# LSH attention and gated MLP on one core: first loads split and reordered, two raw buffers, w_sg and w_out loads held for batch 1

## The chip, the core and the metric

One core of one Trainium2 chip runs the whole kernel. The metric is device microseconds (us) for one execution, as the median of several runs. TensorE (PE) multiplies matrices, VectorE (DVE), ScalarE (ACT) and GpSimd (POOL) work on elements, SyncE (SP) mostly issues DMAs. Each engine executes its own instructions in the order in which they stand in the program, and waits on the others by semaphores.

## The reference, cut

```
q_bits = (einsum('bhsd,dk->bhsk', q, proj) > 0)      # 6 bits; the same for k
mask   = q_bucket[..., :, None] == k_bucket[..., None, :]
scores = where(mask, scale * q @ k.T, -1e9)          # 4 batches, 8 heads, 768 x 768, d 64
attn   = softmax(scores) @ v
x      = attn, heads side by side                    # 4 x 768 x 512
h      = gelu_tanh(x @ w_in); u, v = halves(h)       # 512 -> 2 x 512
v_n    = normalise(v) * g_ln
v_s    = w_sg @ v_n + b_sg                           # over the sequence, 768 x 768
out    = x + (u * v_s) @ w_out
```

All of it is in 32-bit floats.

## The kernel before, in words

**Attention.** The 32 heads are taken as 16 pairs (two heads of 64 columns fill the 128 partitions). For a pair n, `load` fetches q and k (192 KB per head and operand), `values` fetches v, `parts` transposes q and k on PE and splits each into a high and a low part (ACT `h`, DVE `l`), `features` multiplies with the projection matrix and turns signs into the bucket features `f`, `largest` computes a first score and DVE takes the row maxima `mx`, `shift` writes them into the features, and `weigh` computes the scores again in three products, with ACT taking the exponential into a ring of p tiles. The 768 queries of a pair go in two phases (256 and 512 columns). GpSimd, or DVE for some steps of the last pair (`LASTADDS`), adds the p tiles up into `sum`; PE multiplies p with v into `av`. `finish` takes the total of a phase over partitions, sends it through DRAM (s, sq), takes the reciprocal on DVE, sends that through DRAM again (r, rs) and scales: GpSimd `xt`, then DVE `xt`, then the store to `xs`. So 32 phases pass through four DMAs each. The number in a name is the phase: `xt_28` and `sum_56/57` are pair 14's first phase, `xt_30`, `sum_60/61` pair 15's first, `xt_31`, `sum_62/63` the very last. While attention runs, 16 weight jobs (`weight_job`, one row block of w_in each, with the port shared by DVE and GpSimd in mind) prepare w_in in `wflat`.

**Gated MLP.** For each of 4 batches `hidden_v` and `hidden_u` multiply x with w_in in a seven-product scheme: `prepare_ops` splits seven sums of blocks into high and low parts (x into op0 to op6, w_in into w0 to w6), `multiply` runs the products. `gate` and `project` follow for the four batches. w_sg is loaded by `gate_raw` in six groups of four transposing DMAs into one buffer `stg`, each followed by a transposition on DVE; w_out by `out_weights` in eight weight jobs. The op tiles op0 and op1 lie in memory that is free before attention ends; op2 to op6 and the output tiles lie where p tiles and v were, so they wait for attention's last sums.

**What sets the order.** Every piece of work is put into a `Plan` with an engine, an estimated cost and a priority (a number near to a time); `Plan.order` simulates the engines once while the program is built, and emits the instructions in the order of that simulation. A change of a number in the tables at the head of the file (`MX` for the MLP, `AVP`, `WARMUP`, `JOB0` and others for attention) therefore moves instructions on all engines. PE begins with fillers, multiplications of the identity with itself into an unused bank (L683, `WARMUP` of them), placed wherever the simulation sees PE idle in the first microseconds.

The lines that the change touches most: L308 loads `proj`; L469 loads q and k; L479 loads v; L631 adds p tiles; L660 to L665 are the four DMAs of `finish`; L816 makes low parts of w and op; L838 is a product of `hidden_v` or `hidden_u`, L861 a load of x, L902 a load of w_sg, L949 and L999 copies of a product out of its bank.

Of the kernel before, what the change touches and what calls it, by code (L numbers as in the profile page):

```python
# [9 lines left out]
F32 = mybir.dt.float32  # L10
F32R = mybir.dt.float32r
# [10 lines left out]
MX = {'base': 340.0, 'gs': False, 'norm': 'ACT', 'mul': ('DVE', 'POOL', 'POOL', 'POOL', 'DVE', 'POOL', 'POOL', 'DVE'), 'wg': -14.0, 'z0': -2.76, 'ox': -9.0, 'oz': -10.89, 'sp': -10.51, 'ro': -10.87, 'gr': 41.0, 'lx': 7.81, 'lz': -3.23, 'gap': 0.59, 'wo': -58.22, 'ws': 8.72, 'ul': 19.73, 'wi': -125.28, 'x0': -59.43, 'lox': ('DVE', 'DVE', 'DVE', 'DVE', 'DVE', 'DVE', 'DVE'), 'loz': ('DVE', 'DVE', 'POOL', 'DVE', 'DVE', 'DVE', 'DVE'), 'log': ('DVE', 'DVE', 'DVE', 'POOL'), 'low': ('DVE', 'POOL', 'DVE', 'DVE', 'DVE', 'DVE', 'DVE')}  # L22

AVP = 9.58
GY, GX, NPT = (3,), (3, 3), 22
NAV = 1
S0P = 0.39
AHEAD = 8
PREP, SHIFTP, FINP, WSTEP, WP = 0.64, -0.32, 3.66, 14.6, 13.44
# [3 lines left out]
FIRSTP, FIRSTS, FIRSTQ, LATE = -2.54, 2.51, -8.5, 5.81  # L33
LOAD0 = 1.35
PARTP = 1.03
VP, MARK, WARMUP = -20.0, 2, 40
X0P = 313.74
LASTADDS = ["POOL", "POOL", "DVE", "DVE", "DVE"]
AHEAD1 = 3.78
JOB0, JOBS = 1, 115  # L40
# [3 lines left out]
class Plan:  # L44
# [73 lines left out]
    def order(self):  # L118
# [32 lines left out]
        while len(out) < len(G):  # L151
# [14 lines left out]
            t0, e = min((max(when(n), since(n)), e) for e, rs in ready.items() for n in rs if early(n))  # L166
# [77 lines left out]
def kernel(  # L244
# [179 lines left out]
    if True:  # L424
# [36 lines left out]
        def load(n, prio):  # L461
            st = Pair()
            st.n, st.b, st.hp = n, *divmod(n, NP)
            st.raw = []
            for s, (nm, src) in enumerate((("q", q), ("k", k))):
                t = early.ring([P, NT, 2, D], F32, nm, 1)
                for j in range(2):
                    def fn(eng, t=t, j=j, src=src):
                        eng.dma_start(t()[:, :, j, :], src[st.b, 2 * st.hp + j].rearrange("(t p) d -> p t d", p=P))  # L469
                    dma(prio + 0.2 * s, 1.09 if n else LOAD0, fn, w=[(t, j)], e=ACT if n == 0 and s else LOADS)  # L470
# [15 lines left out]
        def parts(st, i, prio):  # L486
# [20 lines left out]
            plan.add(PE, 0.48, prio, tr, [st.raw[s] for s, _ in keys] + [(t, x) for t in (hh, lo) for x in keys] + gate, [tp], form="full")  # L507
# [128 lines left out]
        def finish(st, ph, prio):  # L636
# [4 lines left out]
            h, W = n // 2, n // 64  # L641
            sm, e = late.ring([P, NY], F32, "sm", 3), ps_tile() if st.n < NPAIR - 1 else late.ring([P, WIDE], F32, "e", 2)
# [129 lines left out]
    def w_slot(s):  # L772
        return (r0 if s < 3 else r1).ring([P, NT * HN], F32R, f"w{s}")

    def prepare_ops(left, blk, order, dst, n, a, prio, step, lo_eng):
# [49 lines left out]
    def multiply(order, ni, nc_, lhs, rhs, n, bufs, prio, step, done):  # L825
        a, b, c = {}, {}, {}
        for s, k in enumerate(order):
            group = {1: a, 6: a, 7: a, 4: a, 5: b, 3: b, 2: c}[k]
            for i in range(ni):
# [11 lines left out]
                plan.add(PE, 3 * nc_ * n * 0.0004525, prio + s * step + 0.01 * i, mm, bufs(s), [ps])  # L841
# [25 lines left out]
    def in_weights(prio):  # L867
        w = {s: w_slot(s) for s in range(7)}
        wf = lambda: wflat[:, :NC * FF].rearrange("p (a b) -> p a b", a=NC)
        for u in range(2):  # L870
# [10 lines left out]
            prepare_ops(False, [blk(j, k) for j in range(2) for k in range(2)], GORDER, dst, 512, 2, prio + 8 * u, 1.0, LOW)  # L881
# [11 lines left out]

    def gate_raw(prio):
        wt = plan.buf("wraw", 1)
        sg = w_sg.rearrange("(a b) s -> b a s", b=32)
        for t in range(NT):
            st = r2.ring([P, S], F32, "stg")
            for g in range(4):
# [3 lines left out]
                dma(prio + 3 * t, 0.65, fn, w=[(st, g)])  # L903
# [33 lines left out]
    def hidden_v(b, ops, w, prio, step):  # L937
# [54 lines left out]
        multiply(GORDER, 3, 2, lhs, rhs, QN, lambda s: [(ops[s], 0), (ops[s], 1), (w[s], (0, 0)), (w[s], (0, 1))], prio, step, done)  # L992
# [170 lines left out]
    wi = in_weights(T + M_["wi"])  # L1163
    blk = load_x(0, T + M_["x0"])
    g_col, b_bc = vectors(T + 30)
    for b in range(B):
# [6 lines left out]
        if b == 0:  # L1173
            wt = gate_raw(T + M_["gr"])
# [52 lines left out]
```

## Time and profile before

| | us |
|---|---|
| median of 3 runs | 756.45 (754.81, 756.45, 757.75) |
| the profiled execution, whole | 749.46 |
| its span, first to last instruction | 747.7 |
| TensorE busy in it | 721.7 |

The profiled execution is 7.0 us shorter than the median of the runs; what lies around its span is 1.76 us. Where a row below says how long something takes, it is from that one execution. A line of the timeline view joins instructions of one kind that follow each other: start, length, engine, line, operation, output <- input, count, and in brackets how long the engine had been idle and who released it.

### The profile page before, as it was taken

The numbers are of one execution on the slowest core, as the hardware profiler recorded it, in microseconds if no ns is written. First come the engines' busy times: TensorE is split into PE (matmuls) and PEld (weight loads), VectorE is DVE, ScalarE is ACT, GpSimd is POOL, SyncE is SP. The second block draws the span as 40 slices with busy tenths as digits, with TensorE's granted clock in tenths as the row PEclk, the third lists the DMA queues.
The fourth block names the chain that finished last, engine by engine and source line by source line (L and its number), as shares of the span: only waits on it lengthen the run. The fifth ranks groups of instructions, "written<-read, shape, count | busy, mean of one in ns | idle before, by whom it ended". The sixth has DMA issues, their size and how long they took to land.

```text
span 747.7 us, 16648 instructions
## 1 busy us (share of the span) xinstructions
PE 721.7 (97%) x6396; PEld 579.3 (77%) x6396; DVE 557.7 (75%) x1022; ACT 361.0 (48%) x697; POOL 379.0 (51%) x355
## 2 busy tenths in 40 slices
PE   8999999999999799999999978899999999999997
PEld 8677667676767566867676648899999989999896
DVE  4896878789788989778975967769899845445443
ACT  2355546554655354655565746758769221202010
POOL 0267669678866756967886750211314521304020
PEclk9999999999999899999999998899999999999999
DMA  5333442442344043244122335576544756474534
GB/s 112 74 69 92 96 98 58 112 111 62 99 101 117 21 108 80 79 109 113 26 66 64 89 72 141 156 215 245 191 156 161 244 144 186 104 205 99 143 75 113
DMA packets 200272, 86.04 MB, mean 115 GB/s; under 512 B 171264, under 2 KB 179584, under 8 KB 200192
## 3 DMA queue, kind: packets, MB, share of 16 engines
q1 hardware_dynamic: 197088, 84.18, 43.2%
q10 hardware_dynamic: 3104, 0.80, 0.5%
q8 instruction: 50, 0.82, 0.5%
q14 instruction: 30, 0.25, 0.1%
HBM read 59.48 MB, written 25.36 MB: 113 GB/s over the span
## 4 chain that ended last, share of the span: by engine, by line
PE 74%; DVE 13%; DMA 5%; ACT 3%; issue 3%; POOL 2%; SPq 0%; DVEq 0%; ACTq 0%; POOLq 0%
PE g L596 16%; PE g L1105 13%; PE av L619 10%; PE g L1151 9%; PE g L543 8%; PE g L838 5%; PE g L518 5%; PE av L622 3%; PE g L497 2%; DMA rs<-r 2%; PE g L651 2%; DVE mx L551 1%; PE ftp L683 1%; POOL sum L631 1%; DVE wy L349 1%
## 5 line engine op out<-in xcount | busy, mean ns | idle before, releaser
L601 ACT ACTIVATE p<-g 128x512 f32<-128x512 f32 x288 | 157.4, 599 | 65.0 <-PE g L596 57.1
L631 POOL TENSOR_TENSOR sum<-sum,p 128x512 f32<-128x512 f32 x154 | 183.4, 1226 | 4.1 <-ACT p L601 4.1
L551 DVE TENSOR_REDUCE mx<-g 128x1 f32<-128x512 f32 x192 | 122.7, 684 | 32.7 <-PE g L543 27.9
L631 POOL TENSOR_TENSOR sum<-p,p 128x512 f32<-128x512 f32 x64 | 83.8, 1326 | 87.0 <-ACT p L601 87.0
L1105 PE MATMUL g<-w,op 128*128 128x384 f32 x576 | 100.7, 334 | 0.0
L1105 PEld LDWEIGHTS g<-w,op 128*128 128x128 f32 x576 | 100.0, 188 | 0.2
L619 PE MATMUL av<-p,v 128*32 128x512 f32 x768 | 88.1, 594 | 1.3 <-ACT un L657 1.3
L553 DVE TENSOR_REDUCE mx<-g 128x2 f32<-128x512 f32 x96 | 61.5, 683 | 27.3 <-PE g L543 24.2
L596 PE MATMUL g<-h 64*128 64x256 f32 (+1 forms) x384 | 75.4, 350 | 5.6 <-DVE xt L673 5.0
L838 PE MATMUL g<-w,op 128*128 128x256 f32 x504 | 64.9, 291 | 7.6 <-ACT out L949 5.8
L596 PE MATMUL g<-h,l 64*128 64x256 f32 (+1 forms) x384 | 72.2, 338 | 0.0
L596 PE MATMUL g<-f 64*128 64x256 f32 (+1 forms) x384 | 71.4, 336 | 0.2 <-DMA f<-m 0.2
L838 PEld LDWEIGHTS g<-w,op 128*128 128x128 f32 x504 | 63.5, 198 | 10.0 <-ACT out L949 6.3
L596 PE MATMUL g<-l,h 64*128 64x256 f32 (+1 forms) x384 | 71.1, 335 | 0.0
L543 PE MATMUL g<-f 64*128 64x512 f32 (+1 forms) x384 | 68.8, 347 | 1.0 <-DVE f L523 0.9
L838 PE MATMUL g<-op,w 128*128 128x384 f32 x336 | 64.0, 348 | 3.9 <-ACT out L999 3.4
L1073 POOL TENSOR_TENSOR out<-out,ul 128x384 f32<-128x384 f32 x20 | 20.3, 1017 | 93.4 <-issue 49.9
L543 PE MATMUL g<-h 64*128 64x512 f32 (+1 forms) x384 | 66.6, 336 | 0.0
L672 POOL TENSOR_TENSOR xt<-un,rs 128x256 f32<-128x256 f32 (+1 forms) x32 | 34.3, 1073 | 61.7 <-DMA rs<-r 44.1
L838 PEld LDWEIGHTS g<-op,w 128*128 128x128 f32 x336 | 60.6, 196 | 6.3 <-ACT out L999 5.4
L596 PEld LDWEIGHTS g<-h 64*128 64x128 f32 x384 | 41.8, 187 | 24.2 <-DVE xt L673 5.9
L1151 PE MATMUL g<-woh,op 128*128 128x512 f32 x192 | 59.8, 389 | 0.0
(127 smaller groups left out, 1287.4 us busy)
## 6 DMA issues: line engine op xcount, KB each, us to landing
q<-in_q_dram SPq DMA_DIRECT2D x32, 192.0 KB
v<-in_v_dram SPq DMA_DIRECT2D x16, 384.0 KB
raw<-xs SPq DMA_DIRECT2D x16, 384.0 KB
vn<-out SPq DMA_DIRECT2D x24, 256.0 KB
ud<-out SPq DMA_DIRECT2D x16, 384.0 KB
stg<-xs SPq DMA_DIRECT2D x96, 64.0 KB
ul<-ud SPq DMA_DIRECT2D x32, 192.0 KB
raw<-vn SPq DMA_DIRECT2D x8, 768.0 KB
```

What stands on the lines that cost most here:

```text
L518: nc.tensor.matmul(fp()[:, c * n:(c + 1) * n], w[:, s, :], x()[:, s, cs], start=(u == 0), stop=(u == 2))
L543: nc.tensor.matmul(sc[j]()[:, c * NY:c * NY + b - a], x()[row(j), 0, qs], x()[row(j), 1, a:b], start=(n == 0), stop=(n == 1))
L551: nc.vector.tensor_reduce(mx()[:, 0, i0 + w, j:j + 1], sc[j]()[:, :WIDE], axis=AX.X, op=ALU.max, negate=True)
L553: nc.vector.tensor_reduce(mx()[:, 1, i0:i0 + 2, j], two(sc[j]()), axis=AX.X, op=ALU.max, negate=True)
L596: nc.tensor.matmul(sc[j]()[:, i * w:(i + 1) * w], x()[row(j), 1, ks], y()[row(j), 0, cs], start=(m == 0), stop=(m == 3))
L601: plan.add(ACT, 0.6, prio, lambda j=j: nc.scalar.activation(p[j]()[:, :, :NY], two(sc[j]()), AF.Exp, scale=SCALE), [sc[j]], [p[j]])
L619: nc.tensor.matmul(two(av())[rows(j, a)], st.v()[:, j, x, cols(a)], ps[x][j]()[:, :, :NY], start=(x == 0), stop=(x == 5))
L631: (nc.gpsimd if e == POOL else nc.vector).tensor_add(two(sums[j]()), a, p[j]()[:, :, :NY])
L672: plan.add(POOL, 0.13 + n / 420.0, prio + TAILP, lambda: nc.gpsimd.tensor_mul(xt()[:, :n], un()[:, :n], rs()[:, :n]), [un, rs], [xt])
L838: nc.tensor.matmul(ps()[:, :n], lhs(s, i, ci, x, y), rhs(s, i, ci, x, y), start=(first and ci == 0 and x + y == 0), stop=(ci == nc_ - 1 an ...
L1105: nc.tensor.matmul(ps()[:, :HN], a()[:, x, c0:c0 + P], c()[:, 3 * HN * y + ci * HN:3 * HN * y + (ci + 1) * HN], start=(j == 0 and ci == 0 ...
L1151: nc.tensor.matmul(ps(), a()[:, x, c0:c0 + P], w()[:, 2 * j + ci, :], start=(j == 1 and ci == 0 and x == 0 and w is th), stop=(j == 0 and ...
```

## The change

- **Loads of the first pair.** `proj` is issued by GpSimd's queue instead of SP's. q of pair 0 is loaded in two parts (column tiles 0 and 1, then 2 to 5). ACT's function table is loaded early, by a dummy operation (`warm`).
- **Rings.** q and k have two buffers (`RAWS`) instead of one, and a transposition waits for the halves that it reads. The ring of p tiles has 19 entries instead of 22.
- **Layout.** k and v are read so that one partition holds six consecutive rows (1536 B in a run) instead of rows 128 apart (256 B in a run). The keys are thereby permuted, in k and v alike.
- **Fillers.** 30 instead of 40, and other priorities for the first pairs.
- **w_sg and w_out.** Both wait for buffers `began`: their first loads may be issued when the first product of batch 1 has begun. `gate_raw` is called in batch 1's turn.
- **w_in.** w0 to w2 are prepared as before; the splits for w3 to w6 have priorities of their own (`wj`), later.
- **Last pair.** Its first addition of the second phase goes to DVE instead of GpSimd (`LASTADDS`); the planner takes its DRAM round trips as 1.5 us longer (`TRIP`), which changes the order only.
- **Engines.** Three of seven low parts of x (`lox`: third, sixth, seventh) go to GpSimd, none of w_in's; other tables are retuned.

```diff
-GY, GX, NPT = (3,), (3, 3), 22
+TRIP = 1.5
+RAWS, LATEQ, PRQ = 2, 4.0, True
+GY, GX, NPT = (3,), (3, 3), 19
...
-VP, MARK, WARMUP = -20.0, 2, 40
+VP, MARK, WARMUP = -20.0, 2, 30
...
-LASTADDS = ["POOL", "POOL", "DVE", "DVE", "DVE"]
+LASTADDS = ['DVE', 'POOL', 'DVE', 'DVE', 'DVE']
...
-JOB0, JOBS = 1, 115
+JOB0, JOBS = 2, 114
...
+    warm = const.tile([P, 1], F32, name="warm")
+    nc.scalar.mul(warm, small, 1.0)
     for j in range(2):
-        nc.sync.dma_start(pr[j * D:(j + 1) * D], proj)
+        (nc.gpsimd if PRQ else nc.sync).dma_start(pr[j * D:(j + 1) * D], proj)
...
-                t = early.ring([P, NT, 2, D], F32, nm, 1)
...
+                t = early.ring([P, NT, 2, D], F32, nm, RAWS)
+                for ts in ((slice(0, 2), slice(2, NT)) if n + s == 0 else (slice(0, NT),)):
+                    for j in range(2):
...
+                            order = "(p t) d -> p t d" if src is k else "(t p) d -> p t d"
...
-                st.v(), v[st.b, 2 * st.hp:2 * st.hp + 2].rearrange("j (t p) d -> p j t d", p=P)),
+                st.v(), v[st.b, 2 * st.hp:2 * st.hp + 2].rearrange("j (p t) d -> p j t d", t=NT)),
...
-            prepare_ops(False, [blk(j, k) for j in range(2) for k in range(2)], GORDER, dst, 512, 2, prio + 8 * u, 1.0, LOW)
+            prepare_ops(False, [blk(j, k) for j in range(2) for k in range(2)], GORDER, dst, 512, 2, [prio + s + 8 * u if s < M_["r0n"] else T + M_["wj"] + 15 * u + 2.1 * s for s in range(7)], 0.0, LOW)
...
-                dma(prio + 3 * t, 0.65, fn, w=[(st, g)])
+                dma(prio + 3 * t, 0.65, fn, [began[M_["grb"]]], [(st, g)])
...
-                       lambda x=x: x(), x, p, JOBC)
+                       lambda x=x: x(), x, p, JOBC, [began[M_["wob"]]])
...
-        if b == 0:
+        if b == M_["grb"]:
             wt = gate_raw(T + M_["gr"])
```

Three places in the order show what this does.

**ACT's first instructions** (`k_0` is pair 0's k, `pr` the projection matrix, `pw` its arrangement, `h0_0` the high part of pair 0). Before:

```order
L469 DMA k_0_266<-in_k_dram 128x6x64 x2
L409 ACT_TABLE_LOAD
L409 ACTIVATE pw_117<-pr_73 64x6 x8
L412 CAST pwh_127<-pw_117 128x256
L501 CAST h0_0_299<-g0_850_289 128x2x256
```

After:

```order
L475 DMA k_0_262<-in_k_dram 128x6x64
L310 ACT_TABLE_LOAD
L310 ACTIVATE warm_74<-small_69 128x1
L413 ACTIVATE pw_119<-pr_73 64x6 x4
L475 DMA k_0_262<-in_k_dram 128x6x64
L413 ACTIVATE pw_119<-pr_73 64x6 x4
L416 CAST pwh_129<-pw_119 128x256
L509 CAST h0_0_291<-g0_850_281 128x2x256
```

The second half of k now stands behind four operations that read `pr`.

**GpSimd at the end of attention.** Before:

```order
L631 TENSOR_TENSOR sum_60_6758<-p12_168,p14_170 128x512
L631 TENSOR_TENSOR sum_61_6782<-p13_169,p15_171 128x512
L672 TENSOR_TENSOR xt_28_6823<-un_28_6445,rs_28_6736 128x256
L631 TENSOR_TENSOR sum_60_6758<-sum_60_6758,p0_156 128x512
L631 TENSOR_TENSOR sum_61_6782<-sum_61_6782,p1_157 128x512
L631 TENSOR_TENSOR sum_62_6863<-p6_162,p16_172 128x512
L631 TENSOR_TENSOR sum_63_6884<-p7_163,p17_173 128x512
L631 TENSOR_TENSOR sum_62_6863<-sum_62_6863,p2_158 128x512
L631 TENSOR_TENSOR sum_63_6884<-sum_63_6884,p3_159 128x512
```

After:

```order
L639 TENSOR_TENSOR sum_60_6590<-p16_174,p1_159 128x512
L639 TENSOR_TENSOR sum_61_6595<-p0_158,p2_160 128x512
L639 TENSOR_TENSOR sum_60_6590<-sum_60_6590,p3_161 128x512
L681 TENSOR_TENSOR xt_27_6670<-un_27_6233,rs_27_6592 128x512
L639 TENSOR_TENSOR sum_61_6595<-sum_61_6595,p4_162 128x512
L681 TENSOR_TENSOR xt_28_6737<-un_28_6407,rs_28_6655 128x256
L639 TENSOR_TENSOR sum_62_6725<-sum_62_6725,p13_171 128x512
L639 TENSOR_TENSOR sum_63_6765<-sum_63_6765,p14_172 128x512
```

`xt_28` moved behind the sums of pair 15's first phase, and two additions left the engine.

**SP's queue behind pair 15's totals** (`stg` from `in_moe_w_sg_dram` is w_sg, `raw_1` batch 1's x). Before:

```order
L902 DMA stg_2_6916<-in_moe_w_sg_dram 32x24x32 x4
L665 DMA rs_29_6940<-r_14_1_259 128x1x512
L664 DMA r_15_0_261<-sq_30_6906 128x4
L861 DMA raw_1_6973<-xs_1_94 128x768 x4
L902 DMA stg_3_7003<-in_moe_w_sg_dram 32x24x32
L665 DMA rs_30_7013<-r_15_0_261 128x1x256
L902 DMA stg_3_7003<-in_moe_w_sg_dram 32x24x32 x3
```

After, and then the place where w_sg now begins:

```order
L674 DMA rs_30_6936<-r_15_0_257 128x1x256
L673 DMA r_15_1_259<-sq_31_6907 128x8
L872 DMA raw_1_6971<-xs_1_96 128x768 x4
L684 DMA xs_3_98<-xt_30_6983 128x256
L674 DMA rs_31_7020<-r_15_1_259 128x1x512
```

```order
L915 DMA stg_0_7254<-in_moe_w_sg_dram 32x24x32 x4
L1035 DMA ud_0_103<-out1_0_6901 128x768 x3
L348 DMA ow64_0_7311<-in_moe_w_out_dram 128x512
L1035 DMA ud_0_103<-out1_0_6901 128x768
L1083 DMA ul_0_7341<-ud_0_103 128x384
L915 DMA stg_1_7350<-in_moe_w_sg_dram 32x24x32 x4
L872 DMA raw_2_7377<-xs_2_97 128x768 x4
```

All six groups of w_sg moved behind the last pair's round trips, and two of them now stand ahead of batch 2's x.

## Rows read from the trace of the kernel before

**Rows 1.** The page: busy us, share of span, instructions by engine

```profile
PE 721.7 (97%) x6396; PEld 579.3 (77%) x6396; DVE 557.7 (75%) x1022; ACT 361.0 (48%) x697; POOL 379.0 (51%) x355
```

**Rows 2.** Windows: length, PE, PEld, DVE, ACT, POOL busy, clock, DMA share, GB/s

```profile
420.00:460.00 40.00, 32.28 (x297) 24.62 (x298) 32.14 (x39) 23.48 (x47) 19.88 (x13) 0.91 0.34 70
460.00:500.00 40.00, 35.79 (x234) 34.29 (x235) 27.76 (x61) 25.96 (x52) 7.15 (x9) 0.91 0.60 171
```

**Rows 3.** Timeline of the start, all engines

```profile
0.74 1.22 SPq L308 DMA_DIRECT2D pr<-in_proj_dram  x2
0.74 1.03 ACTq L469 DMA_DIRECT2D k<-in_k_dram  x2
...
2.79 6.96 PE L683 MATMUL ftp<-ident 128*128 128x128 f32 x34 [0.26 <-DVE fcol L401]
3.71 1.28 ACT L409 ACT_TABLE_LOAD   x1 [3.71 <-DMA pr<-in_proj_dram]
5.00 1.25 ACT L409 ACTIVATE pw<-pr 64x6 f32<-64x6 f32 x8
...
9.59 0.38 PE L497 MATMUL g<-ident,q 128*128 128x128 f32 x2
...
16.98 2.40 PE L683 MATMUL ftp<-ident 128*128 128x128 f32 x20
```

**Rows 4.** Timeline: the stall inside attention, and its operation 103 us earlier

```profile
144.19 0.30 DVE L349 TENSOR_SCALAR wy<-w 128x256 int32<-128x256 int32 x1
...
247.13 8.96 DVE L349 TENSOR_SCALAR wy<-w 128x256 int32<-128x256 int32 x1
...
248.44 4.65 POOL L631 TENSOR_TENSOR sum<-sum,p 128x512 f32<-128x512 f32 x4
...
256.99 1.39 PE L596 MATMUL g<-h 64*128 64x512 f32 x2 [5.05 <-DVE xt L673]
```

**Rows 5.** PE's timeline through the four batches of hidden

```profile
438.10 4.58 PE L838 MATMUL g<-w,op 128*128 128x256 f32 x36
...
450.83 10.02 PE L838 MATMUL g<-w,op 128*128 128x256 f32 x60 [5.76 <-ACT out L949]
...
473.74 11.43 PE L838 MATMUL g<-op,w 128*128 128x384 f32 x48 [2.34 <-ACT out L999]
...
517.48 15.27 PE L838 MATMUL g<-w,op 128*128 128x256 f32 x126
532.59 14.97 PE L838 MATMUL g<-op,w 128*128 128x384 f32 x84
547.40 15.62 PE L838 MATMUL g<-w,op 128*128 128x256 f32 x126
...
579.83 4.49 PE L1105 MATMUL g<-w,op 128*128 128x384 f32 x25
```

**Rows 6.** DVE's timeline: attention's last sums

```profile
446.42 2.44 DVE L631 TENSOR_TENSOR sum<-sum,p 128x512 f32<-128x512 f32 x4
```

**Rows 7.** GpSimd's timeline at attention's end

```profile
435.44 1.28 POOL L672 TENSOR_TENSOR xt<-un,rs 128x256 f32<-128x256 f32 x1 [5.32 <-DMA rs<-r]
...
440.41 2.54 POOL L631 TENSOR_TENSOR sum<-p,p 128x512 f32<-128x512 f32 x2
```

**Rows 8.** The chain that ended last, near attention's end: start, us, what

```profile
453.43 7.25 DMA r<-sq
460.75 8.12 DMA rs<-r
...
496.62 4.16 DMA raw<-xs
```

**Rows 9.** SP's queue near attention's end

```profile
430.08 0.58 SPq L665 DMA_DIRECT2D rs<-r  x1
431.15 3.70 SPq L902 DMA_DIRECT2D stg<-in_moe_w_sg_dram  x4
...
461.34 6.13 SPq L902 DMA_DIRECT2D stg<-in_moe_w_sg_dram  x3
```

More of the change, by code (lines that the diff above doesn't have):

```diff
@@ L19 @@
 DRAM = bass.MemoryType.DRAM
-MX = {'base': 340.0, 'gs': False, 'norm': 'ACT', 'mul': ('DVE', 'POOL', 'POOL', 'POOL', 'DVE', 'POOL', 'POOL', 'DVE'), 'wg': -14.0, 'z0': -2.76, 'ox': -9.0, 'oz': -10.89, 'sp': -10.51, 'ro': -10.87, 'gr': 41.0, 'lx': 7.81, 'lz': -3.23, 'gap': 0.59, 'wo': -58.22, 'ws': 8.72, 'ul': 19.73, 'wi': -125.28, 'x0': -59.43, 'lox': ('DVE', 'DVE', 'DVE', 'DVE', 'DVE', 'DVE', 'DVE'), 'loz': ('DVE', 'DVE', 'POOL', 'DVE', 'DVE', 'DVE', 'DVE'), 'log': ('DVE', 'DVE', 'DVE', 'POOL'), 'low': ('DVE', 'POOL', 'DVE', 'DVE', 'DVE', 'DVE', 'DVE')}
-AVP = 9.58
-GY, GX, NPT = (3,), (3, 3), 22
+MX = {'r0n': 3, 'base': 340.0, 'gs': False, 'norm': 'ACT', 'mul': ('DVE', 'POOL', 'POOL', 'POOL', 'DVE', 'DVE', 'POOL', 'POOL'), 'wg': -6.88, 'z0': -13.06, 'ox': -18.52, 'oz': -10.9, 'sp': -11.69, 'ro': -9.67, 'gr': -9.1, 'lx': 3.63, 'lz': -3.11, 'gap': 10.9, 'wo': -29.13, 'ws': 8.55, 'ul': 17.78, 'wi': -129.15, 'x0': -64.01, 'lox': ('DVE', 'DVE', 'POOL', 'DVE', 'DVE', 'POOL', 'POOL'), 'loz': ('DVE', 'POOL', 'DVE', 'POOL', 'DVE', 'DVE', 'DVE'), 'log': ('DVE', 'DVE', 'POOL', 'DVE'), 'low': ('DVE', 'DVE', 'DVE', 'DVE', 'DVE', 'DVE', 'DVE'), 'grb': 1, 'wob': 1, 'wj': -19.12}
+AVP = 9.56
+TRIP = 1.5
+RAWS, LATEQ, PRQ = 2, 4.0, True
+GY, GX, NPT = (3,), (3, 3), 19
 NAV = 1
-S0P = 0.39
+S0P = 0.76
 AHEAD = 8
-PREP, SHIFTP, FINP, WSTEP, WP = 0.64, -0.32, 3.66, 14.6, 13.44
+PREP, SHIFTP, FINP, WSTEP, WP = 0.65, -0.56, 4.02, 14.6, 13.43
 LOADS = "SP"
@@ L164, in early @@
                 return not wants[n] or e not in first or first[e] == n
-            t0, e = min((max(when(n), since(n)), e) for e, rs in ready.items() for n in rs if early(n))
+            t0, _, e = min((max(when(n), since(n)), e != "POOL", e) for e, rs in ready.items() for n in rs if early(n))
             if t0 > 1e8:
@@ L465, in load, with fn @@
             for s, (nm, src) in enumerate((("q", q), ("k", k))):
-                t = early.ring([P, NT, 2, D], F32, nm, 1)
[L467 to L470, printed above, removed]
+                t = early.ring([P, NT, 2, D], F32, nm, RAWS)
+                for ts in ((slice(0, 2), slice(2, NT)) if n + s == 0 else (slice(0, NT),)):
+                    for j in range(2):
+                        def fn(eng, t=t, j=j, src=src, ts=ts):
+                            order = "(p t) d -> p t d" if src is k else "(t p) d -> p t d"
+                            eng.dma_start(t()[:, ts, j, :], src[st.b, 2 * st.hp + j].rearrange(order, p=P)[:, ts])
+                        cost = 0.95 if s else 1.2 if n else LOAD0 * (ts.stop - ts.start) / NT
+                        dma(prio + 0.2 * s + (LATEQ if ts.start else 0), cost, fn, w=[(t, (ph, j)) for ph in range(2) if ts.start <= 2 * ph < ts.stop],
+                            e=ACT if n == 0 and s else LOADS)
                 st.raw.append(t)
@@ L506, in parts @@
             gate = [st.mark] if st.n == 0 and i == 2 else []
-            plan.add(PE, 0.48, prio, tr, [st.raw[s] for s, _ in keys] + [(t, x) for t in (hh, lo) for x in keys] + gate, [tp], form="full")
+            plan.add(PE, 0.48, prio, tr, [(st.raw[s], (ph, j)) for s, ph in keys for j in range(2)] + [(t, x) for t in (hh, lo) for x in keys] + gate, [tp], form="full")
             plan.add(ACT, 0.6, prio, high, [tp], [(hh, x) for x in keys])
@@ L641, in finish @@
             h, W = n // 2, n // 64
+            trip = TRIP if st.n == NPAIR - 1 else 0.0
             sm, e = late.ring([P, NY], F32, "sm", 3), ps_tile() if st.n < NPAIR - 1 else late.ring([P, WIDE], F32, "e", 2)
@@ L772, in w_slot @@
     def w_slot(s):
-        return (r0 if s < 3 else r1).ring([P, NT * HN], F32R, f"w{s}")
+        return (r0 if s < M_["r0n"] else r1).ring([P, NT * HN if M_["gs"] else 2048 if s > 3 else NT * HN], F32R, f"w{s}")
     def prepare_ops(left, blk, order, dst, n, a, prio, step, lo_eng):
@@ L791, in prepare_ops @@
         tt = (tmp, [t])
+        prios = prio if isinstance(prio, list) else [prio] * 7
         for s, k in enumerate(order):
+            prio = prios[s]
             src = {1: b11, 2: b12 if left else b21, 3: b12 if left else b22, 4: b22 if left else b21,
@@ L892, in vectors @@
         return g_col, b_bc
+    began = [plan.buf(f"began_{b}", 1) for b in range(B)]
     def gate_raw(prio):
```

32 lines of the change are left out of this document (16 added, 16 removed).

## The prediction

> **What bounds the kernel now.** The page comes first: TensorE is busy 721.7 of 747.7 us [rows 1], so all that the change can win lies in the 26 us in which PE stands and in the stretches in which it works slowly. Three places hold nearly all of it. (a) *The start.* The timeline shows 34 filler products (17 fillers) from 2.79 to 9.75, and the first real transposition only at 9.59, though q, k and the projection matrix are asked for at 0.74 [rows 3]. (b) *The stall inside attention.* One DVE instruction of a weight job takes 8.96 us where the same one took 0.30 us 103 us earlier; GpSimd adds p tiles back to back beside it. PE stands 5.05 us behind it and then needs 1.39 us for two products that elsewhere take 0.39 to 0.40 [rows 4]. I put the place at 7.2 us: 5.05, and 2.2 for the slow rows. (c) *The change to the MLP.* The four batches of hidden lie between 438.10 and 579.83, 141.7 us. A batch that nothing disturbs is 126 and 84 products, from 517.48 to 547.40, 29.9 us [rows 5]; four make 119.7. So 22 us are lost (some 3 of them to totals and first gate products), and 79.4 − 59.8 = 19.5 of them in the first two batches, 438.10 to 517.48. In these two windows the granted clock is 0.91 on average [rows 2], so PE runs part of them at the lower of its two levels: 60 products of 256 columns take 10.02 us behind a wait of 5.76, where 60 at the pace of 126 in 15.27 are 7.27 [rows 5]. A wait here thus costs about one and a half times its length: 5.76 + 2.75 = 8.5. Everything else, the steady part of attention and the gate, keeps PE without a gap; only fewer instructions would shorten it, and the change leaves the products as they are. The ring of 19 p tiles, the second buffer for q and k, and the layout of k and v lie beside that: I take 0.
>
> **Start, −2.0.** q's first third is asked for ahead of all else, `proj` no longer stands ahead of it, and 5 fillers instead of 17 stand ahead of the first transposition. What comes last now is the second half of k: it stands on ACT behind four of the eight `pw` operations (1.25 for eight), which wait for `pr`; the table load (1.28) no longer does. `pr` was asked for at 0.74 and landed by 3.71, 3.0 later [rows 3]. So 3.7 + 0.6 + 0.5 for the issue (1.03 for two) + 3.0 to land = 7.8, against 9.59. Of these 1.8 I take 1.0 for the earlier beginning (bounds: loses 0.1, wins 2.2) and 1.0 more for fillers and gaps behind it (20 filler products at 16.98 cost 2.40 [rows 3]; bounds −2 to +2.3, since fewer fillers can leave PE at the lower clock level). Together: from 2 us worse to 4.5 better.
>
> The Trainium skill (DMA: Bandwidth & Descriptors, "Specifications") speaks against GpSimd's queue here: it gives about 1 us to the first byte for a transfer issued by GpSimd and about 0.6 for one by SyncE or ScalarE. By it the start would gain 1.6 instead of 2.0, an estimate from that page; no run here shows it yet.
>
> **Attention's last sums, −6.6.** PE's wait of 5.76 at 450.83 is for ACT's copy of a product out of its bank; ACT is held by casts of op tiles, and those by memory that is free only when the last sums are done, at 446.42 + 2.44 = 448.86 [rows 5, 6]. Back from there: GpSimd stood 5.32 us until `rs_28` landed, with `xt_28` ahead of pair 15's sums, and did two p,p additions (2.54) that the change hands to DVE [rows 7]. Now `xt_28` stands behind them. So 5.3 + 2.5, less 1.2 for the two additions on DVE (four sums took 2.44 [rows 6]): the sums end 6.6 us earlier. What PE can get back there is at most 8.5 (above). Against full pay, PE now takes the totals ahead of every product of hidden, so that the 36 products that it did at 438.10 (4.58) no longer cover the wait [rows 5]. Bounds: 1.3 (xt_28's wait only moves ahead of the second phase's sums) to 7.9.
>
> **Chain behind the sums, −3.0.** The last pair's round trips go by SP's queue between groups of w_sg: r to sq took 7.25 and rs to r 8.12 [rows 8], while `rs_28`, issued at 430.08, landed at 435.44, 5.36 [rows 7, 9]. Without w_sg in the queue (3.70 for four loads, 6.13 for three [rows 9]) I take half of 8.12 − 5.36, 1.4, and half of 7.25 − 4, 1.6 (4 is what a load of x took [rows 8]); half, because PE has other products to do meanwhile. PE's wait of 2.34 at 473.74 [rows 5] is of this kind. Bounds 0 to 6.
>
> **w_in's operations moved, +2.4.** Seven DVE operations of 128x512 (five low parts, a sum and a difference) move from ahead of the last sums to behind them; at 2.44 / 4 = 0.61 [rows 6] that is 4.3 us, with their waits at most 4.8, just where DVE makes op tiles. Against it GpSimd, else free there, takes three of seven op low parts. Half: 2.4, bounds 0 to 4.8.
>
> **Batches 1 to 3, −1.3.** 2.5 us of loss lie behind 517.48 (62.35 − 59.84 [rows 5]) and more in batch 1. Against a gain stands the load of w_sg, that is now there: six groups through one buffer, each waiting for DVE's transposition of the one ahead, with batch 2's and 3's x among them on SP's queue. Bounds: 3.3 gained to 6 lost; the loss's full price is rival C.
>
> **Stall, 0.** Six weight jobs in before reach DVE in a stretch where GpSimd adds; one starved. After has four or so such places; nothing in the rows says which starve. I let the 7.2 stand, with bounds 0 and 14.4.
>
> Sum: −2.0 − 6.6 − 3.0 + 2.4 − 1.3 = −10.5. The profiled execution took 749.46, 7.0 less than the median of 756.45; it would come to 739.0, and the median to 756.45 − 10.5 = **746.0**.
>
> **Rivals.** *A: the stall goes as well.* Other work stands in DVE's row at every such place, so chance decides whether the 8.96 recurs. It gives 746.0 − 7.2 = 738.8. For it: five of six places in before cost nothing, as 0.30 shows [rows 4]. Against: the jobs' places are as exposed as ever. The rule of the Trainium skill (SBUF — State Buffer, "SBUF: two separate sides") goes this way: DVE and GpSimd arbitrate for one pair of ports, and who starts first holds it for the whole instruction. By it a DVE instruction would wait for one addition, 4.65 / 4 = 1.2 us; the row shows one that waited through several, so the trace shows the rule's cause and not its length.
>
> *B: what the last phase wins is given back.* rs_28 holds GpSimd ahead of the second phase's sums instead (gain 1.3, not 6.6), and the start keeps its time: 746.0 + 5.3 + 2.0 = 753.3, no change by the bound below. For it: GpSimd still has `xt_28` in front of two additions for the last sums. Against: DVE's reciprocal for it now stands ahead of the four w_in operations instead of behind them.
>
> *C: slower, by the late x.* In after, `raw_2` stands on SP behind `stg_0` and `stg_1`, `raw_3` among the last groups. Batch 1 then begins at about 477 (485 in before less the gains) and ends on PE 29.9 later, 507. A group of w_sg at 3.70, the wait for its landing and transposition, the second group, and a load of x (4.16 [rows 8]) come to about 501 with DVE's preparation: some 5.5 us to spare. At 6.13 for three loads [rows 9], 8.2 a group, it is 9 us more, and decides from 2.8 more for each group. Then batch 2 starts late, and batch 3 likewise: up to two waits of 7 at one and a half times, 21 us: 746.0 + 21 − 7 (that the early trips still save) = 760. Against it: the 6.13 fell where the queue was shared with round trips.
>
> **How the numbers follow.** Forecast 0.42, A 0.25, B 0.18, C 0.09; 0.06 for others, most of them better (all bounds on the good side: 732). What is within 0.5% (3.8 us), about what a measurement of this kernel can tell from no change, is 752.7 to 760.2. Faster: the forecast, A and most of the others, 0.74; same: B, 0.17; slower: C, 0.09. The range leaves C and half the others out, and reaches from A's 738.8, with 2.5 more for a start at its good bound, to B's 753.3 with 2 for a start at its bad one: 736 to 755.
>
> **What would show it.** In the profile of the changed kernel: first transposition at 7.5 to 8.5; last sums done by about 442 on the old clock; no wait of PE over 3 us behind them; rs to r under 6.5 in the chain; batch 0 from attention's end to batch 1's first product under 40 us (47 in before); no wait of PE on DVE at the start of batches 2 and 3. It is wrong if PE waits for a load of x, if a weight job takes over 5 us more than once, or if DVE's operations on w_in hold up the first op tiles for more than 4.8.

## The result, and the profile after

The changed kernel takes **748.14 us** (median of 4: 746.84 to 750.10), the kernel before 756.14 beside it (754.81 to 757.75): a ratio of 0.9895, with a 95% interval of 0.9863 to 0.9928. 746.0 was forecast, with 736 to 755 around it. The profiled executions stand closer together: 746.84 against 749.46 whole, spans 745.1 against 747.7.

That number needs one plain sentence beside it: on three other chips the kernel before took 738.0 to 743.2 us in 43 runs, 744.5 to 748.8 in 21 and 753.9 to 754.5 in 2, while the changed kernel, on one of these, took 748.19 again, there 0.9% more than the 740.59 of before. So the gain of 1% holds against the long runs of before on the first chip, and not in general. Why is told below.

By stage (PE's timeline: end of the last product of p and v; end of the last product of hidden; end of the span):

| | before | after | difference |
|---|---|---|---|
| attention, to the end of `av` | 438.2 | 443.9 | +5.7 |
| from there to the end of hidden | 141.8 | 131.9 | −9.9 |
| gate, project and tail | 167.7 | 169.3 | +1.6 |
| span | 747.7 | 745.1 | −2.6 |

One line of before belongs to the table. Nine products of the gate stand ahead of the end of hidden there, and behind it in the changed kernel:

```profile
574.10 1.72 PE L1105 MATMUL g<-w,op 128*128 128x384 f32 x9
575.66 0.51 PE L838 MATMUL g<-op,w 128*128 128x384 f32 x2
```

They take 1.56 us, from 574.10 to 575.66, and account for the +1.6 of the last stage. So hidden itself, without them, is 8.3 us shorter, not 9.9.

The page's busy times answer to [rows 1]:

```profile
PE 719.5 (97%) x6376; PEld 570.4 (77%) x6376; DVE 554.0 (74%) x1009; ACT 362.5 (49%) x698; POOL 406.4 (55%) x367
```

The waits of PE (waiter <- waited for: total us, times, longest):

```profile
PE g L604 <- DVE mx L559: 7.3, 4, 4.6
PE g L505 <- DMA k<-in_k_dram: 3.2, 1, 3.2
...
PE g L849 <- DVE out L965: 2.0, 1, 2.0
PE g L849 <- ACT out L1012: 1.6, 2, 1.3
PE g L849 <- DVE op L827: 1.4, 1, 1.4
PE g L660 <- DVE sum L639: 1.2, 1, 1.2
```

The wait of 5.76 us for ACT [rows 5] is gone; in its place stand one of 1.2 for the last sums and three of 2.0 and less on DVE and ACT. But attention has four waits for DVE's maxima where before had one stall, and the start has a new one for k.

PE's timeline at the transition answers to [rows 5], DVE's to [rows 6]:

```profile
445.08 1.23 PE L660 MATMUL g<-sum,ones 128*32 128x256 f32 x8 [1.18 <-DVE sum L639]
446.24 2.49 PE L849 MATMUL g<-w,op 128*128 128x256 f32 x18
...
452.42 0.74 PE L849 MATMUL g<-w,op 128*128 128x256 f32 x4 [1.37 <-DVE op L827]
454.06 0.98 PE L849 MATMUL g<-w,op 128*128 128x256 f32 x6 [0.91 <-DVE xt L682]
457.00 4.40 PE L849 MATMUL g<-w,op 128*128 128x256 f32 x24 [1.96 <-DVE out L965]
...
483.83 0.87 PE L849 MATMUL g<-w,op 128*128 128x256 f32 x6
```

```profile
440.75 4.88 DVE L639 TENSOR_TENSOR sum<-sum,p 128x512 f32<-128x512 f32 x6
```

The last sums end at 445.63, 1.7 us behind PE's last product of p and v; before, at 448.86, 10.7 behind it. Batch 1's first product stands at 483.83, 39.9 behind the end of `av` (before: 46.8). The granted clock over batch 0 is 0.96 (443.90 to 483.80), before 0.85 (438.20 to 485.00). No wait is over 2 us, and none is for a load of x.

### The profile page after: what moved, and what is told of

Read it like the earlier page. It is cut to its first block, busy times and chain, and to the rows that moved or that the text cites. A ratio compares the mean times of both kernels' runs of the same rounds, so it can differ in the third digit from the quotient of the medians.

```text
span 745.1 us, 16622 instructions
## 1 busy us (share of the span) xinstructions
PE 719.5 (97%) x6376; PEld 570.4 (77%) x6376; DVE 554.0 (74%) x1009; ACT 362.5 (49%) x698; POOL 406.4 (55%) x367
## 4 chain that ended last, share of the span: by engine, by line
PE 71%; DVE 15%; DMA 8%; issue 2%; POOL 2%; SPq 1%; ACT 1%; ACTq 0%; DVEq 0%; POOLq 0%
PE g L604 15%; PE g L1118 13%; PE g L1164 9%; PE g L551 8%; PE av L627 7%; PE g L849 7%; PE av L630 5%; PE g L526 3%; PE g L505 2%; DMA w<-in_moe_w_in_dram 2%; DVE mx L559 2%; DMA rs<-r 2%; PE g L660 2%; DVE mx L561 1%; DVE wx L356 1%
## 5 line engine op out<-in xcount | busy, mean ns | idle before, releaser
L639 POOL TENSOR_TENSOR sum<-sum,p 128x512 f32<-128x512 f32 x154 | 180.4, 1204 | 11.6 <-ACT p L609 11.6
L639 POOL TENSOR_TENSOR sum<-p,p 128x512 f32<-128x512 f32 x62 | 81.5, 1335 | 66.3 <-ACT p L609 66.2
L627 PE MATMUL av<-p,v 128*32 128x512 f32 x768 | 85.9, 594 | 0.4 <-ACT un L666 0.4
L551 PE MATMUL g<-f 64*128 64x512 f32 (+1 forms) x384 | 70.4, 354 | 0.0
L1086 POOL TENSOR_TENSOR out<-out,ul 128x384 f32<-128x384 f32 x20 | 24.4, 1219 | 77.6 <-DVE out L1084 37.6
L627 PEld LDWEIGHTS av<-p,v 128*32 128x32 f32 x768 | 23.2, 110 | 53.6 <-issue 51.9
L849 PE MATMUL g<-op,w 128*128 128x384 f32 x336 | 60.9, 337 | 1.7 <-ACT out L1012 1.6
L849 PEld LDWEIGHTS g<-op,w 128*128 128x128 f32 x336 | 57.7, 188 | 3.4 <-ACT out L1012 2.5
```

Of the source, the lines that this page charges most:

```text
L551: nc.tensor.matmul(sc[j]()[:, c * NY:c * NY + b - a], x()[row(j), 0, qs], x()[row(j), 1, a:b], start=(n == 0), stop=(n == 1))
L627: nc.tensor.matmul(two(av())[rows(j, a)], st.v()[:, j, x, cols(a)], ps[x][j]()[:, :, :NY], start=(x == 0), stop=(x == 5))
L639: (nc.gpsimd if e == POOL else nc.vector).tensor_add(two(sums[j]()), a, p[j]()[:, :, :NY])
L849: nc.tensor.matmul(ps()[:, :n], lhs(s, i, ci, x, y), rhs(s, i, ci, x, y), start=(first and ci == 0 and x + y == 0), stop=(ci == nc_ - 1 an ...
L1086: sub(M_["mul"][2 * f + h], HN, p, lambda e: e.tensor_mul(at(f, h), at(f, h), ul()), [k, ul], [k])
```

## The experiments

Times beside each other in a paragraph are from one chip, where nothing else is said.

**The recurring waits, and the changed kernel beside before.** The changed kernel unaltered, on another chip.

> The changed kernel unaltered, beside the kernel before on one chip. On the chip of the last runs before took 744.5 (738.8 to 754.5 in 23 runs), on the first one 756. My theory: before's time moves with the number of places where a weight job starves DVE, the changed kernel's does not (its four waits of PE for DVE's maxima, 7.3 us in all, come from its order and recur); so 746 to 750 here too, and the same four waits in its profile; against before about 0.5% slower to 0.5% faster. Rival: the change is worth 1% on every chip; then 736 where before takes 744.

748.19 (747.55 to 749.24 in 7 runs); before 740.59 (738.17 to 746.88 in 15); ratio 1.0091, interval 1.0053 to 1.0130. The same four waits for the maxima stand in its profile (6.8 us), at the same pairs within 2 us. The first theory held, by more than it said: here the change is a loss. Where the wait comes from, DVE's timeline of the changed kernel shows, with GpSimd's and SP's beside it:

```profile
209.78 0.47 DVE L359 SCALAR_TENSOR_TENSOR wy<-w,wy 128x256 f32<-128x256 uint32 x1
...
216.22 0.29 DVE L353 TENSOR_SCALAR wy<-w 128x256 int32<-128x256 int32 x1 [2.82 <-DMA w<-in_moe_w_in_dram]
216.55 0.72 DVE L354 SCALAR_TENSOR_TENSOR wx<-w,wy 128x256 int32<-128x256 int32 x1
217.38 1.33 DVE L356 SCALAR_TENSOR_TENSOR wx<-wg,wx 128x256 f32<-128x256 f32 x1
218.74 1.24 DVE L358 TENSOR_SCALAR wy<-wx 128x256 int32<-128x256 int32 x1
220.02 1.28 DVE L359 SCALAR_TENSOR_TENSOR wy<-w,wy 128x256 f32<-128x256 uint32 x1
221.33 1.28 DVE L360 TENSOR_TENSOR wflat<-wx,wy 128x256 f32<-128x256 f32 x1
```

```profile
216.95 2.88 POOL L639 TENSOR_TENSOR sum<-p,p 128x512 f32<-128x512 f32 x2
219.79 2.54 POOL L639 TENSOR_TENSOR sum<-sum,p 128x512 f32<-128x512 f32 x2
```

```profile
210.60 0.38 SPq L348 DMA_DIRECT2D w<-in_moe_w_in_dram  x1
```

The rows of w_in have one buffer, and DVE reads it for the job ahead until 210.25. The load for this job is issued at 210.60, and the first operation on it begins 5.6 us later; DVE stands 2.82 for it. The job's operations, late, then run side by side with GpSimd's additions: each takes about as long as one addition (1.24 to 1.33, additions 1.27 to 1.44) instead of 0.3 to 0.5. The maxima stand behind them on DVE, and PE, for 4.6 us, behind the maxima. Two of the other three waits follow jobs with late loads too (1.09 and 0.42 us late), the fourth (0.45) does not.

The Trainium skill (SBUF — State Buffer, "SBUF: two separate sides") says that of a DVE and a GpSimd operation which contend, the one that starts first holds the shared pair of ports for its whole instruction and the other blocks. In these rows each of four DVE operations takes about one addition, which agrees. The 8.96 of [rows 4], several additions long, is more than one instruction's wait.

**Two buffers for the rows of w_in**, in the changed kernel, in the kernel before, and in the changed kernel with the totals put back (that run, alone, comes further below):

```
-            return early.ring(shape, dt, tag)
+            return early.ring(shape, dt, tag, 2 if tag == "w64" else 1)
```

> The changed kernel with two buffers instead of one for the rows of w_in that a weight job reads, so that a load need not wait for the job ahead of it; on SP's queue the loads move 10 to 15 us ahead of their jobs. In the changed kernel's profile DVE waited 2.82 us for such a load at 216.22 (1.09 and 0.42 at two other jobs); the job then met GpSimd's additions, each of its operations took 1.3 instead of 0.3 to 0.5, and PE waited 4.56 for the maxima behind it. My theory: the late load is the cause of the waits that recur; without it three of four vanish, and the 1.5 to 7 us that these pairs took longer, so 738 to 741 where the changed kernel took 748. Rival: the jobs meet the additions all the same, by their place on DVE; then 746 to 749.

744.15 (742.90 to 745.85 in 11 runs), 1.0044 of before's 740.46 (1.0024 to 1.0064). On other chips the changed kernel took 748.1 and 748.2. The cause of these waits is borne out, the price was not (738 to 741 was expected). DVE's waits for loads of w_in are gone (4.3 us in three places in the changed kernel), and PE's list reads

```profile
PE g L604 <- ACT p L609: 4.3, 2, 2.5
...
PE g L604 <- DVE mx L559: 0.9, 3, 0.3
```

in place of 7.3 for the maxima; but 4.3 us for ACT's exponentials are new (the run before_totals, below, shows waits of this kind), so 4 us come of it and not 7 to 10. The places of the jobs on DVE moved together with the loads; what the loads alone did isn't shown apart.

> The kernel before with two buffers for the rows of w_in. In before the stall of its profile was a weight job's first operation, 8.96 us long with its data there long before (its load was issued 8.8 us earlier), beside additions on GpSimd. My theory: that stall is not from a late load, so the second buffer doesn't take it away by itself; times still fall into steps of about 7 us (739, 746, 754), with other places exposed. Rival: it is a late load as well; then all runs lie within 2 us, at 738 to 740.

738.16 to 754.45 in 12 runs (745.00), in steps as foretold: 5 at 738 to 739, 4 at 744 to 748, 3 at 753 to 754. So before's stall isn't a late load: the second buffer leaves the steps, and in [rows 4] the operation itself is long, it does not wait for its data. The profiled run fell on a step without a stall: `av` ends at 429.8, hidden 138.9 later, span 736.4. Beside it the changed kernel's first profile, of another chip, is 14.1 us longer in attention, 7.0 shorter to the end of hidden and 1.6 longer behind it: 8.7 in all. That is why the change loses where before runs without a stall.

> Both edits in one: two buffers for the rows of w_in and the priority of the totals put back (FINP 3.66). The changed kernel with the totals put back took 741.9 and showed no stall, with 107 moves between tile shapes; here there are 116, since the order moved. If the waits for late loads are what the second buffer takes away, there is nothing left to take here: 741 to 743. Rival: some of the 741.9 is still late loads; then under 740.

738.32 (736.49 to 741.49 in 12 runs), 0.9970 of before (0.9944 to 0.9996): the rival was nearer. It is the fastest kernel tried, 0.3% under before's median on that chip, and its runs lie within 5 us where before's spread over 10. Before's lower step there (22 of 28 runs, 738.0 to 743.2) has its median 1.5 us above it. `av` ends at 434.7, hidden 131.8 later: attention is 9.2 shorter than in the changed kernel, and hidden keeps its gain.

**The weight jobs left out.** The conversion of w_in is replaced by a copy of half of the words on ScalarE:

```
+        if src is w_in:
+            plan.add("ACT", 0.4, prio, lambda: nc.scalar.copy(dst(), w()[:, :, 1].bitcast(F32)), [w], [(buf, (c, f0))])
+            return
```

> The kernel before, with the conversion of w_in left out: each of its 16 weight jobs copies half of the words by one instruction on ScalarE instead of six on DVE and one on GpSimd (so hidden and all that follows work on other numbers). It tells what the weight jobs cost attention in the timed runs. My theory: the timed runs of before, 7 us above the profiled one, hold more stalls of the kind that the profile shows once (7.2 us); then 742, that is 14 under 756. Rival: they hold one or none, and the 7 us are something else; then 749 or more.

738.99; 11 of 12 runs lie between 737.8 and 739.8, one at 747.5, where before spread from 738.8 to 754.5 beside it. So the steps of before come with the weight jobs, all but one run's; which operation of a job makes a step, these runs don't show. The forecast of 742 came from the 756 of the first chip; on this one before's lower step is 739 and the jobs' price is the spread above it. `av` ends at 428.9 here, 9.3 us ahead of before's profile with its one stall (of another chip).

> The changed kernel with the conversion of w_in left out in the same way as in the run of the kernel before without it (one copy on ScalarE for each weight job, so hidden and what follows work on other numbers). That run took 739.0 and its profile 737.2. My theory: without stalls the changed kernel still loses 0.28 us a pair (4 us) in attention and wins some 9 at the transition; so 734, 5 under before without the conversion. Rival: the gain of the change is only that it has fewer stalls; then the same, 739.

746.98 (744.73 to 751.43 in 9 runs), where 734 was expected: both theories fell. The waits for the maxima are gone, but PE waits three times for ACT's exponentials (6.3 us), and `av` ends at 447.2. The order differs everywhere, since the copies now stand on ACT; the run says nothing on what the jobs cost in the changed kernel.

**The steady part: 25.77 instead of 25.49 us a pair.** The rows of the second-phase totals in the timelines of before (L651), after and, as the third, the kernel below with the steady numbers put back:

```profile
81.47 0.61 PE L651 MATMUL g<-sum,ones 128*32 128x256 f32 x8
106.96 0.61 PE L651 MATMUL g<-sum,ones 128*32 128x256 f32 x8
132.46 0.61 PE L651 MATMUL g<-sum,ones 128*32 128x256 f32 x8
```

```profile
85.16 0.64 PE L660 MATMUL g<-sum,ones 128*32 128x256 f32 x8
110.96 0.64 PE L660 MATMUL g<-sum,ones 128*32 128x256 f32 x8
136.72 0.64 PE L660 MATMUL g<-sum,ones 128*32 128x256 f32 x8
```

```profile
86.43 0.61 PE L660 MATMUL g<-sum,ones 128*32 128x256 f32 x8
111.93 0.62 PE L660 MATMUL g<-sum,ones 128*32 128x256 f32 x8
137.43 0.61 PE L660 MATMUL g<-sum,ones 128*32 128x256 f32 x8
```

Steps of 25.49 and 25.50, of 25.80 and 25.76, of 25.50 again. PE shows no wait in these stretches. What differs is what stands beside the total, here in the changed kernel and in before:

```profile
110.75 0.28 PE L604 MATMUL g<-f 64*128 64x256 f32 x2
110.96 0.64 PE L660 MATMUL g<-sum,ones 128*32 128x256 f32 x8
111.53 0.50 PE L551 MATMUL g<-f 64*128 64x512 f32 x2
111.87 0.40 PE L551 MATMUL g<-h 64*128 64x512 f32 x2
```

```profile
106.96 0.61 PE L651 MATMUL g<-sum,ones 128*32 128x256 f32 x8
107.40 1.47 PE L619 MATMUL av<-p,v 128*32 128x512 f32 x12
```

Between score products (tiles of 64 rows) the total takes 0.57 from its start to the next row's, and the first score row behind it 0.34; between products of p and v (tiles of 32 columns, as its own) the total takes 0.44, and a score row of that size is 0.23 elsewhere. With 0.09 ahead of it that is 0.33 us for two changes of tile shape. In the order of the programs PE changes shape 93 times in before's attention and 121 times in the changed kernel, two for each pair more.

> The changed kernel with the planner's numbers for the steady part of attention put back (totals, p times v, turns between tile shapes, landing, weight jobs, first pair): 91 moves between tile shapes instead of 120, second-phase totals again between p times v. It keeps the two buffers for q and k, 19 p tiles, the layout of k and v, the loads of the first pair, the hold of w_sg and w_out, and the tables of the MLP. My theory: a pair takes 25.5 us again, attention is 4 us shorter, stalls come and go as in before; 737 to 745, under the changed kernel. Rival: the longer pair comes from the 19 tiles, the layout or the second buffer; then a pair stays at 25.8.

The edit, cut (it also puts back the first pair's numbers, `AVP`, `JOB0`, `JOBS`, two of the planner's weights for changes of tile shape, and its rule for ties):

```
-PREP, SHIFTP, FINP, WSTEP, WP = 0.65, -0.56, 4.02, 14.6, 13.43
+PREP, SHIFTP, FINP, WSTEP, WP = 0.64, -0.32, 3.66, 14.6, 13.44
...
-    LAND = 0.54
+    LAND = 1.29
```

The pair is 25.50 with 19 tiles, two buffers and the new layout in place: this rival fell. `av` ends at 439.6, 6.0 earlier than in the changed kernel on that chip (445.6). But the kernel takes 758.64 (737 to 745 was expected): hidden ends 141.8 behind `av`, as in before, and gate, project and tail take 177.6, 8.3 more. The order of those stages changed with the numbers, which the expectation left out; which of them did it, the run doesn't show.

> The changed kernel with that one number put back (FINP 4.02 to 3.66): 107 moves between tile shapes instead of 121. My theory: 14 moves at 0.14 us are 2 us, so about 746, and pairs in which the totals stand beside p times v take 25.5. Rival: no difference, 748.

The edit is FINP alone, of the lines above. 741.89 (741.24 to 746.49 in 12 runs), 0.9996 of before beside it (0.9964 to 1.0028); no wait for the maxima over 0.2 us in its profile. That is 6 and not 2 us under the changed kernel's 748 of two other chips. Attention ends at 432.4, 11.5 earlier than in the changed kernel's first profile, with one late load of 0.97 us left, since the order of the weight jobs moved too; but hidden ends 137.7 behind it, 5.8 more. So one number of the planner takes back more than half of what the transition had won. Four late pairs, with the totals between products of p and v, take 25.44 to 25.52; the eight before them, with first-phase totals now between scores, 25.8 on average.

> The kernel before with one number of the change alone: the priority of a phase's totals (FINP 3.66 to 4.02). On PE it only moves the totals of most pairs from beside the p times v products to a place between score products, so that PE goes 28 times more often from products of one tile shape to another (93 times before, 121 here, 121 in the changed kernel). My theory: each such move costs 0.14 us, which is what the changed kernel loses per pair (25.77 against 25.49 us with PE never idle); so about 4 us slower than before, 760, and a pair takes 25.75 to 25.8 in its profile. Rival: the longer pair comes from something else of the change (19 p tiles, the layout of k and v, transpositions among the feature products); then this kernel is within 1 us of before and a pair stays at 25.5.

```
-PREP, SHIFTP, FINP, WSTEP, WP = 0.64, -0.32, 3.66, 14.6, 13.44
+PREP, SHIFTP, FINP, WSTEP, WP = 0.64, -0.32, 4.02, 14.6, 13.44
```

789.95, 1.062 of before: 45 us, not 4. The run shows something else than it was made for. PE's list, and ACT's timeline at the second of these waits:

```profile
PE g L596 <- ACT p L601: 22.9, 12, 2.6
```

```profile
116.83 0.69 ACT L671 ACTIVATE g<-rs,less 128x512 f32<-128x512 f32 x1 [2.25 <-DMA rs<-r]
117.46 1.07 ACT L601 ACTIVATE p<-g 128x512 f32<-128x512 f32 x2
```

With a later total its DRAM round trip ends later, and ACT's copy of `rs` (L671), which waits for it, stands ahead of the exponentials that PE waits for. The changed kernel has the same later totals without these waits; its other numbers were moved along. PE's waits here, 22.9 for ACT and 4.8 for the maxima, are not the whole of the 45; the rest is left open. The rate can't be read from this run.

**The transition.** Two edits of the changed kernel: w_sg and w_out without their wait for batch 1, and the first additions of the last phase on GpSimd again.

```
-                dma(prio + 3 * t, 0.65, fn, [began[M_["grb"]]], [(st, g)])
+                dma(prio + 3 * t, 0.65, fn, [], [(st, g)])
...
-                       lambda x=x: x(), x, p, JOBC, [began[M_["wob"]]])
+                       lambda x=x: x(), x, p, JOBC, [])
```

> The changed kernel without the wait for batch 1: the loads of w_sg and w_out may be issued as in the kernel before, and the first groups of w_sg again stand among the last pair's round trips on SP's queue. My theory of the transition: the round trips get longer again (rs from r 6 to 8 us instead of about 5), batch 0 loses up to 3 us, and the rest of the gain there (the last sums, earlier by the order on GpSimd and DVE) stays; 748 to 751. Rival: the hold is what the whole gain of the transition comes from; then 755 or more. Second rival: it is worth nothing, 748.

752.83 (750.04 to 755.29 in 6 runs); the changed kernel took 748.1 and 748.2 on two other chips. That is above the 748 to 751 expected. Hidden ends 134.5 behind `av`, against 131.9 and 131.4 with the hold: 2.6 to 3.1 us. The rest stays without it, so both rivals fell. But the theory of the round trips fell as well. Batch 1's first product stands 40.7 behind `av` (39.9 and 39.3 with the hold), so only 0.8 to 1.4 of it is lost in batch 0 and the larger part in batches 1 to 3. And rs follows r after 1.9 us in pair 15's first phase and after 9.7 in the last:

```profile
454.50 0.33 SPq L673 DMA_DIRECT2D r<-sq  x1
...
456.44 0.55 SPq L674 DMA_DIRECT2D rs<-r  x1
459.05 0.32 SPq L673 DMA_DIRECT2D r<-sq  x1
...
466.87 1.86 SPq L915 DMA_DIRECT2D stg<-in_moe_w_sg_dram  x3
468.77 2.83 SPq L674 DMA_DIRECT2D rs<-r  x1
```

No load of w_sg came back between the first two, so this run does not restore the queue of the kernel before.

```
-LASTADDS = ['DVE', 'POOL', 'DVE', 'DVE', 'DVE']
+LASTADDS = ["POOL", "POOL", "DVE", "DVE", "DVE"]
```

> The changed kernel with the first additions of the last phase put back on GpSimd (LASTADDS), all else as it is: xt_28 then stands on GpSimd ahead of two additions of the last sums, and DVE has two additions less. My theory of the transition: the last sums end 1 to 3 us later, PE waits that much longer ahead of hidden's first product (1.2 us in the changed kernel); 749 to 751. Rival: these two additions hang on xt_28's round trip, not on who makes them, and nothing moves: 748.

751.71 against 748.19 for the changed kernel on the same chip, 3.5 us; hidden ends 135.0 behind `av`. That is a little above the 749 to 751 expected, and not by the way that was expected: PE's wait for the last sums is hardly longer (1.3); the time is lost behind it, where PE waits 2.0 for GpSimd's low part of an op tile and 2.3 for ACT's casts. So who makes these additions counts, and through what stands behind them on GpSimd.

**The start.** The projection matrix on SP's queue again (PRQ False):

> The changed kernel with the projection matrix on SP's queue again, ahead of q. In the changed kernel it was issued on GpSimd at 1.31 (behind the identity's memory set) and landed 3.1 us later; ScalarE then issues k's second half at 4.76, and PE waits 3.2 us for it, till 9.47. My theory: on SP it is issued at 0.74 and lands by 3.7, k's half goes out 0.8 us earlier and PE begins with k at about 8.7, but q's first third comes 1.2 later; the whole is 0.3 to 0.8 us shorter, which these runs can't tell from none, and the profile's first transposition of k shows it. Rival: q's delay is what counts, and k begins no earlier than 9.5.

747.25 (744.76 to 748.25 in 6 runs), not to be told from the changed kernel's 748.1 and 748.2 on two other chips. The first transpositions of k, in the changed kernel and here:

```profile
9.47 1.51 PE L505 MATMUL g<-ident,k 128*128 128x128 f32 x6 [3.22 <-DMA k<-in_k_dram]
```

```profile
8.84 1.52 PE L505 MATMUL g<-ident,k 128*128 128x128 f32 x6 [3.12 <-DMA q<-in_q_dram]
```

0.6 us earlier, as expected (8.7). In both, PE waits over 3 us with its fillers used up, and these transpositions run at half pace (six in 1.51, where six take 0.82 at 18.45).

## Why the prediction was right, and where it was not

**The transition** came out at its size, −8.3 (−9.9 less the 1.6 of gate products) for the −6.6 − 3.0 + 2.4 − 1.3 = −8.5 forecast, and one of its mechanisms was read rightly. The last sums end 9.0 us nearer to the end of `av`, not 6.6, and the wait of 5.76 went with them; after_last gives 3.5 us back by itself. That a wait costs more than its length agrees with the granted clock over batch 0, 0.85 before and 0.96 after.

The term for the chain, −3.0, has nearly its size in after_nohold (2.6 to 3.1) and not its reason. In the changed kernel r of pair 15's first phase, issued at 452.48, lets rs be issued at 455.50, 3.0 us for the 7.25 of [rows 8]; but that trip is as short without the hold. And the last rs waits on SP behind the load of x, goes out 8.5 us after its r, and lands another 10.2 later, where under 6.5 was to be seen:

```profile
452.48 0.32 SPq L673 DMA_DIRECT2D r<-sq  x1
...
455.50 0.55 SPq L674 DMA_DIRECT2D rs<-r  x1
457.08 0.32 SPq L673 DMA_DIRECT2D r<-sq  x1
463.08 1.94 SPq L872 DMA_DIRECT2D raw<-xs  x4
465.13 0.38 SPq L684 DMA_DIRECT2D xs<-xt  x1
465.60 0.53 SPq L674 DMA_DIRECT2D rs<-r  x1
```

```profile
465.60 10.21 DMA rs<-r
```

The moved operations of w_in cost at most what DVE's waits show, 1.37 + 0.91 + 1.96 = 4.2, within the 0 to 4.8 but above the 2.4 taken; w_in's operations stand ahead of the first of these waits, and x's own ahead of the other two. Batches 1 to 3 take 91.9 us from 483.83 on, 2.2 more than three undisturbed ones; in before 95.0, of which 1.6 are the gate's. That is a gain of 1.5 for the 1.3 taken. Rival C fell, no batch waits for x. (Its 760 lay within the 752.7 to 760.2 that the prediction itself called no change, and the 0.74 for faster is at least 0.01 more than its parts.)

**The steady part**, taken as 0, was the failed step. "The change leaves the products as they are" counted the products and not the order in which they stand: 0.28 us a pair for 13 pairs is 3.6. after_steady shows what stands in its place: with fewer changes of tile shape a pair is back at 25.50. The order of the changed kernel has these changes in it, outside the three places that I chose.

**The stall**, taken as 0 net, is the second. By the steps of the second-phase totals, before's four pairs around its stall and its slower places take 9.2 us more than four at 25.49, the changed kernel's four slow pairs (27.50, 32.89, 27.31, 27.33) 12.0 more than four at 25.77: +2.7. I asked whether jobs stand beside additions, and didn't follow the job's load back to its one buffer and SP's queue. Rival A fell too: the waits recur, in both profiles of the changed kernel. The job at 216.22 takes 6.4 us and the one at 348.28 5.2 (with other operations between); more than one job over 5 us was a sign named for being wrong.

**The start**, −2.0, is the third: it won nothing. In the first 60.00 us PE does the same products in both kernels, count for count (48 of p and v with 512 columns, 24 transpositions of q and 24 of k, and so on), the fillers aside. The first transposition of q moved ahead, from 9.59 to 5.62, but that of k stands at 9.47, with a wait of 3.2 us, where 7.5 to 8.5 was to be seen for the first. k's second half, issued at 4.76, landed 4.6 us later and not 3.0, with q's later loads and the next pair's k (on SP from 4.15, into the second buffer) under way beside it, and PE has no fillers left. Also, q was not asked for at 0.74 in the kernel before, as the prediction says, but at 2.00. What remains of attention's +5.7 after 3.6 and 2.7, −0.6, thus falls in the later pairs.

**The sum** was −10.5 and the profiles differ by 2.6; the medians by 8.0. For the profiled execution 739.0 was forecast, and 746.84 came. That 748.14 lies close to 746.0 is luck: it comes from the runs of before on that chip, 5 to 8 us above their own profiled execution. They lie just above the uppermost step of the other chips' runs. Whether they held another stall each, no profile of theirs can show; that is left open.

## What to carry to other kernels

Where a planner orders the program, a retuned number is a new order everywhere: read PE's order for changes of tile shape, and each waiting instruction for what is queued behind it, in all stages, and not only where the diff has its name. A gain against a kernel whose own time comes in steps holds for the step: count the steps over many runs and chips before a per cent is believed. And a load with one buffer is late where the jobs that use it come close together, as at 210.60 here.

## What was not expected of the hardware

- Two changes of tile shape on PE cost 0.28 to 0.33 us together, with no wait in the profile's list.
- A GpSimd addition and a DVE operation side by side alternate, 1.24 to 1.33 us each, where DVE's alone takes 0.3 to 0.5; once, in before, one DVE operation took 8.96 through several additions.
- The kernel before, unaltered, took 738.0 to 754.5 on three chips in steps of about 7 us, and 754.8 to 757.8 on a fourth. The granted clock of a run falls with its step: 0.990 to 0.995 up to 743.2, 0.985 to 0.993 up to 748.8, 0.984 at 754. In before's profile it is 0.55 from 257 to 262, behind the stall of 5.05 us, and 1.00 again from 262 on, so a stall costs more than its wait.
